# Causal attention with a soft mixture of experts: one transpose of the maxima for a pair of heads, and a rearranged opening

## Chip, cores and metric

The kernel runs on one core of one Trainium2 chip. The metric is the device time of one execution in microseconds (us). Before the change it is 418.62 us, the median of three runs (418.21 to 418.80).

## What is computed

The inputs q, k and v have 8 batches of 12 heads, 448 positions and 64 channels, in float32. A causal attention comes first; its result, with the heads side by side, is x of 3584 rows by 768. A soft mixture of 8 experts with 4 slots each follows.

```python
scores = scale * np.matmul(q, k.transpose(0, 1, 3, 2))
scores = np.where(mask, -1000000000.0, scores)      # mask: above the diagonal
scores = scores - np.max(scores, axis=-1, keepdims=True)
attn = np.exp(scores)
attn = attn / (np.sum(attn, axis=-1, keepdims=True) + 1e-09)
x = np.matmul(attn, v)
...
logits = x @ phi
d = softmax of logits over the rows; slot_input = d.T @ x
slot_out[e] = np.maximum(slot_input[e] @ w1[e], 0.0) @ w2[e]
c = softmax of logits over the slots; out = c @ slot_out
```

## The kernel before

The 96 heads are taken as 48 pairs. `block(p)` (from line 507) is the work around pair p: the last step of the scores of its heads a = 2p and a + 1, the first steps of the scores of the next pair's heads a + 2 and a + 3, and the attention's product with v for pair p. Every instruction is kept in the order in which the program is written, on its own engine (`_InOrder`, line 55), so the order of the calls in `block` is the order in each engine's queue. All instructions therefore carry line 65 in the profile; the tile names tell them apart.

The scores stand transposed in PSUM, keys on the partitions, one 1024-column tile `s` per head, three of them in turn. A head's way through the engines, by the names of functions and tiles:

- `cast_q`, `cast_k` (ScalarE) round q and k to the matmul's type into `qd` and `ks`; `sub_q`, `sub_k` (GpSimd, a few at the start on VectorE) put the rounding's remainder into the upper partitions of `r2` and `ks`; `copy_k2` (ScalarE) copies the rounded keys into `k2`. Remainder and rounded part together make the product exact enough.
- `scores1` (line 249, TensorE): six matmuls. The parts "c03" and "c12" add the causal mask with a bf16 identity (`s<-tri,identb`, 192 and 256 columns), the parts "k3" to "k0" are the product of 64, 192, 320 and 448 columns (`s<-qd,ks`). `scores1_all` fixes their order.
- `max_keys` (line 279, VectorE): k = 0 is the large transposing maximum of the 1024 columns of `s` (`TRANSPOSE_TENSOR_REDUCE r<-s`), k = 1 and 2 are two small maxima over blocks of keys (`TENSOR_REDUCE r<-r`).
- `max_row` (line 300): k = 0 transposes the tile `r` on TensorE (`rt<-ident,r`), k = 1 takes the last maximum of four groups, negated, on VectorE (`mr<-rt`). `rt` and the transposed x (`xm`) share one PSUM bank.
- `max_spread` (line 311, GpSimd): spreads `mr` by a select onto 14 rows of `r2` (`r<-mr` in the profile).
- `scores2` (line 322, TensorE): four matmuls (`s<-r,k`) that subtract the maximum and add the remainders; then `exps` (ScalarE, `pt<-s`).
- `attv` and `attv3` (TensorE, `po<-va,pt`): the product with v. `attv` is called once per head for the first three blocks of queries, `attv3` does the last block for both heads. `norm` (VectorE) divides by the sum into `x`.

In a steady block TensorE's queue is: scores2 of a, scores1 of a + 2, scores2 of a + 1, scores1 of a + 3, attv of a, rt of a + 2, attv of a + 1, attv3, rt of a + 3, then pieces of the mixture (its logits, or the products for the slots, another kind in each of six consecutive blocks), then the four transposes `xm` of the pair before. VectorE's is: the last of `norm` for the pair before, the three `max_keys` of a + 2, the large one of a + 3, mr of a + 2, the small two of a + 3, mr of a + 3, the first steps of `norm`, the mixture's sums. GpSimd's is: sub_q, sub_k, the two spreads.

Behind the last block the expert weights that did not fit beside the attention are loaded, and the experts and the combination run (from line 699). Lines 173 to 181 and 474 to 505 are the opening: the first loads, the first heads' work, and matmuls without use (`warm`, line 213) in the waits.

Of the kernel before, what the change touches and what calls it, by code (L numbers as in the profile page):

```python
# [9 lines left out]
F32 = mybir.dt.float32  # L10
# [16 lines left out]
NQB = S // 32  # L27
# [4 lines left out]
NHD = 2 * NPAIR  # L32
NR, XB, XT = 2, 3, 2
# [2 lines left out]
HT = 2  # L36
WN, PAD = 1536, 168
WARM = (2, 5, 2, 3, 3)
START = (8, 4)


FILL = 9
# [3 lines left out]


SC0, SC1, SC2, SC3 = 576, 0, 320, 512
RW, RC, RF = 96, 4, 20
NQ = 2 * NCH - 1  # L50
CQ0 = (0, 128, 256, 384)
SCOL = (SC0, SC1, SC2, SC3)
# [28 lines left out]
def attention_soft_moe(ctx: ExitStack, tc: tile.TileContext, qk, va, phi, w1, w2, out):  # L81
    nc = _Core(tc)
# [18 lines left out]
    r2_ = [fix.tile([P, 2, S], F32R, name="r20")]  # L101
# [4 lines left out]
    r_ = [fix.tile([P, RW], F32, name=f"r{i}") for i in range(2)]  # L106
# [11 lines left out]

    st = {}

    def load_qk(p, a, hs=slice(0, 2)):
        if p < NPAIR:
            if hs.start == 0:

                st["raw", a, p] = (wres.tile([P, 2 * WN], F32, tag="w", name=f"qk{a}_{p}")[:, 0:2 * S]
                                   .rearrange("p (h s) -> p h s", h=2)
                                   if (p, a) in ((1, 0), (2, 1)) else
                                   raw.tile([P, 2, S], F32, tag="qk", name=f"qk{a}_{p}"))
            nc.sync.dma_start(out=st["raw", a, p][:, hs], in_=qk[p, :, a, hs])

    def loads_v(p, eng=nc.sync):
        if p < NPAIR:
# [39 lines left out]

    for hs in (slice(0, 1), slice(1, 2)):
        load_qk(0, 1, hs)
        load_qk(0, 0, hs)
    load_qk(1, 1)
    load_qk(1, 0)
    loads_v(0)
    load_qk(2, 1)
    load_qk(2, 0)  # L180
# [22 lines left out]
    for i in range(NR):  # L203
        nc.gpsimd.memset(r2_[i][0:64, :, :].bitcast(F32), 0.0)
        nc.vector.memset(ks_[i][:, 2 * S:2 * S + KP].bitcast(F32), 0.0)
        nc.vector.memset(r_[i], -3.0e38)
# [36 lines left out]
    def sub_q(p, hs=slice(0, 2), eng=None):  # L243
        if p < NPAIR:
            (eng or nc.gpsimd).tensor_tensor(out=r2_[p % NR][64:P, hs], in0=st["raw", 0, p][64:P, hs],
                                             in1=qd_[p % NR][64:P, hs], op=ALU.subtract)


    def scores1(i, part):
        if i >= NHD:  # L250
            return
        p, h = divmod(i, 2)
        ks, qd = ks_[p % NR], qd_[p % NR]
        if ("s", i) not in st:
            st["s", i] = s_[i % 3]
            st["open"] = set()
        s = st["s", i]

        bank = part in ("c12", "k1", "k2")
        start = bank not in st["open"]  # L260
        st["open"].add(bank)
        if part[0] == "k":
            c = int(part[1])
            o, w, m = S * h + P * c, S - CQ0[c], min(P, S - P * c + (KP if i else 0))
            nc.tensor.matmul(s[0:m, SCOL[c]:SCOL[c] + w], ks[:, o:o + m],
                             qd[:, h, CQ0[c]:S], start=start, stop=False, skip_group_check=True)
            return
        if part == "c12":
            o = s[:, SC1:SC1 + 2 * SC2].rearrange("p (a n) -> p a n", n=SC2)[:, :, 0:P]
            mask = tri.unsqueeze(1).to_broadcast([P, 2, P])  # L270
        else:
            o, mask = s[:, SC3:SC3 + AW + P], tri2
        nc.tensor.matmul(o, identb, mask, start=start, stop=False, skip_group_check=True)

    def scores1_all(i):
        for part in ("c03", "c12", "k3", "k2", "k1", "k0"):
            scores1(i, part)

    def max_keys(i, k):

        if i >= NHD:
            return
        r = r_[i % 2]
        if k == 0:
            nc.vector.tensor_reduce(out=r[:, RC:RC + 72].rearrange("p (a b)->p a b", b=36)[:, :, 0:16],
                                    in_=st["s", i].rearrange("p (a b k)->p a b k", a=2, k=32),
                                    axis=AX.X, op=ALU.max, apply_transpose=True)  # L290
        elif k == 1:
            w = r[:, 0:84].rearrange("p (j q)->p q j", j=2)[:, 0:16]
            nc.vector.tensor_reduce(out=r[:, RF:RF + 76].rearrange("p (a q)->p a q", a=2)[:, :, 0:8],
                                    in_=w.rearrange("p (a q) j->p a q j", a=2), axis=AX.X, op=ALU.max)
        else:
            nc.vector.tensor_reduce(out=r[:, RF + 8:RF + NQB],
                                    in_=r[:, 14:80].rearrange("p (j q)->p q j", j=3)[:, 0:6],
                                    axis=AX.X, op=ALU.max)

    def max_row(i, k, w=RW - RF, to=None):  # L300
        if i >= NHD:
            return
        if k == 0:
            st["rt", i] = misc(f"rt{i}") if to is None else to
            nc.tensor.transpose(out=st["rt", i][0:w, 0:P], in_=r_[i % 2][:, RF:RF + w], identity=ident)
        else:
            mr = st["mr", i] = wk.tile([NQB, 32], F32, tag="mr", name=f"mr{i}", bufs=2)
            nc.vector.tensor_reduce(out=mr, in_=st.pop(("rt", i))[0:NQB, 0:P].rearrange("p (g t)->p t g", g=4),
                                    axis=AX.X, op=ALU.max, negate=True)

    def max_spread(i):
        if i >= NHD:
            return
        p, h = divmod(i, 2)
        mr = st.pop(("mr", i))

        nc.gpsimd.affine_select(out=r2_[p % NR][0:NQB, h].rearrange("p (b t)->p b t", t=32),
                                in_=mr.unsqueeze(1).to_broadcast([NQB, NQB, 32]),
                                compare_op=ALU.is_equal, fill=0.0, base=0,
                                pattern=[[-1, NQB], [0, 32]], channel_multiplier=1)  # L320

    def scores2(i, cs):
        if i >= NHD:
            return
        p, h = divmod(i, 2)
        s = st["s", i]
        k2, r2 = k2_, r2_[p % NR]
        for c in cs:
            o, w, m = S * h + P * c, S - CQ0[c], min(P, S - P * c + (KP if i else 0))
# [152 lines left out]
        nc.vector.memset(t, v)  # L482
    sub_q(0, h0)
    scores1_all(0)
    warm(START[1])
    for k in range(3):
        max_keys(0, k)
    cast_k(0, h1)
    cast_q(0, h1)
    sub_k(0, h1)  # L490
    nc.gpsimd.memset(si, 0.0)
    max_row(0, 0)
    max_row(0, 1)
    max_spread(0)
    scores1_all(1)
    cast_k(1, h0)
    cast_k(1, h1)
    cast_q(1, h0)
    sub_k(1, h0)
    sub_k(1, h1)  # L500
    for k in range(3):
        max_keys(1, k)
    sub_q(0, h1, nc.vector)
    for hf in range(2):
        nc.sync.dma_start(out=phis[hf], in_=phi[:, 3 * hf:3 * hf + 3])

    def block(p):
# [18 lines left out]
            xcopy(p - 2)  # L526
        scores1_all(a + 2)
        if p == 0:
            max_row(1, 0)
            max_row(1, 1)  # L530
            max_spread(1)
        for k in range(3):
            max_keys(a + 2, k)
        if p == 0:
# [3 lines left out]
        if p == 0:  # L538
            cast_k(2, h1)
        scores1_all(a + 3)  # L540
        max_keys(a + 3, 0)
        sub_q(p + 1)
        load_qk(p + 3, 0)
        if p:
            sub_k(p + 2)
            load_qk(p + 4, 1)
        if m6 == 2 and p > 6:
            logits_d(b, lt)
        copy_k2(p + 1)
# [16 lines left out]
            return  # L566
        for h in range(2):
            attv(a + h, [(qc, 3 * h + qc, FULL) for qc in range(3)], po2, begun)
            if h == 0:
                max_row(a + 2, 0, AW)  # L570
        max_row(a + 2, 1)
        max_spread(a + 2)
        for k in (1, 2):
            max_keys(a + 3, k)
        if p == 0:
            sub_k(2, eng=nc.vector)
            load_qk(4, 1)
# [351 lines left out]
```

## Time and profile before

| | before |
|---|---|
| median of three runs | 418.62 us |
| the profiled execution: time, span | 418.81 us, 417.1 us |
| mean granted TensorE clock | 0.974 |
| busy: TensorE, its weight load | 383.6 us (92%), 300.0 us (72%) |
| busy: VectorE, ScalarE, GpSimd | 295.2, 283.0, 263.3 us (71, 68, 63%) |
| opening: first scores2 of pair 0, of pair 1 | 9.66 us, 20.57 us |
| six consecutive steady blocks (107.57 to 145.81 us) | 38.24 us |
| from 318 us to the end (417 us) | DMA share about 1, 399 to 416 GB/s |

The span is the time from the first to the last instruction on the core; the execution's own time is 1.7 us longer. Busy shares are means over stages with different limits, so the stages are read apart. In rows of the timeline the first two numbers are start and length in us; a bracket at the end has the idle time of that engine just before, and what ended it. Rows with several instructions show the first one's shape. A matmul's end is modelled, so the starts are what counts on TensorE.

### The profile page before, as it was taken

The numbers are of one execution on the slowest core, as the hardware profiler recorded it, in microseconds if no ns is written. First come the engines' busy times: TensorE is split into PE (matmuls) and PEld (weight loads), VectorE is DVE, ScalarE is ACT, GpSimd is POOL, SyncE is SP. The second block draws the span as 40 slices with busy tenths as digits, with TensorE's granted clock in tenths as the row PEclk, the third lists the DMA queues.
The fourth block names the chain that finished last, engine by engine and source line by source line (L and its number), as shares of the span: only waits on it lengthen the run. The fifth ranks groups of instructions, "written<-read, shape, count | busy, mean of one in ns | idle before, by whom it ended". The sixth has DMA issues, their size and how long they took to land.

```text
span 417.1 us, 14076 instructions
## 1 busy us (share of the span) xinstructions
PE 383.6 (92%) x5710; PEld 300.0 (72%) x5710; DVE 295.2 (71%) x827; ACT 283.0 (68%) x402; POOL 263.3 (63%) x212
## 2 busy tenths in 40 slices
PE   7799999999999999999999999999998998997840
PEld 3678888888887888888888878888886644633420
DVE  6687777878877878888788778788884576433540
ACT  5677878877978888788779788887863111432430
POOL 6498898888888888988888888889862000000000
PEclk9699999999999999999999999999999999999975
DMA  7578787788777787677887777877849999999997
GB/s 275 183 228 263 251 261 224 256 260 270 236 232 243 254 283 242 224 257 247 261 270 238 230 242 255 291 236 245 278 156 415 405 426 427 421 417 415 397 394 319
DMA packets 34479, 119.16 MB, mean 286 GB/s; under 512 B 3824, under 2 KB 8944, under 8 KB 32880
## 3 DMA queue, kind: packets, MB, share of 16 engines
q1 hardware_dynamic: 34272, 118.01, 80.3%
q8 instruction: 45, 0.74, 0.7%
q10 hardware_dynamic: 144, 0.27, 0.2%
q14 instruction: 18, 0.15, 0.1%
HBM read 107.25 MB, written 11.01 MB: 284 GB/s over the span
## 4 chain that ended last, share of the span: by engine, by line
PE 78%; DVE 7%; DMA 5%; issue 3%; ACT 2%; POOL 1%; SPq 0%; DVEq 0%; POOLq 0%
PE s L65 34%; PE po L65 25%; PE xm L65 7%; PE rt L65 5%; DMA w<-in_w_dram 4%; PE so L65 2%; PE hp L65 2%; PE pp L65 2%; DVE lm L65 2%; DMA qk<-in_qk_dram 2%; DVE lg L65 1%; PE cp L65 1%; DVE r L65 1%; PE e L65 1%; DVE mr L65 1%
## 5 line engine op out<-in xcount | busy, mean ns | idle before, releaser
L65 ACT ACTIVATE pt<-s 128x1024 f32<-128x1024 f32 x96 | 98.8, 1030 | 53.5 <-PE s L65 49.9
L65 DVE TRANSPOSE_TENSOR_REDUCE r<-s 128x32 f32<-128x1024 f32 x96 | 119.5, 1245 | 20.9 <-PE s L65 18.4
L65 PE MATMUL po<-va,pt 128*64 128x65 f32 x3040 | 111.1, 226 | 0.0
L65 PEld LDWEIGHTS po<-va,pt 128*64 128x64 f32 x3040 | 97.8, 139 | 17.9 <-issue 11.9
L65 POOL TENSOR_TENSOR r<-qk,qd 64x896 fp32r<-64x896 f32 (+1 forms) x48 | 100.4, 2092 | 4.7 <-ACT qd L65 0.9
L65 POOL TENSOR_TENSOR ks<-qk,ks 64x896 fp32r<-64x896 f32 (+1 forms) x48 | 97.9, 2041 | 0.8 <-ACT ks L65 0.8
L65 POOL TENSOR_SCALAR_AFFINE_SELECT r<-mr 14x448 fp32r<-14x448 f32 x96 | 61.6, 642 | 46.2 <-DVE sm L65 26.6
L65 PE MATMUL s<-qd,ks 128*128 128x448 f32 (+4 forms) x384 | 79.8, 331 | 1.5 <-POOL ks L65 1.5
L65 PE MATMUL s<-r,k 128*128 128x448 f32 (+3 forms) x384 | 65.0, 292 | 1.4 <-POOL r L65 1.4
L65 PEld LDWEIGHTS s<-r,k 128*128 128x128 f32 (+1 forms) x384 | 59.6, 177 | 4.5 <-POOL r L65 2.3
L65 PEld LDWEIGHTS s<-qd,ks 128*128 128x128 f32 (+2 forms) x384 | 51.0, 180 | 1.7 <-POOL ks L65 1.7
L65 ACT ACTIVATE ks<-qk 128x896 fp32r<-128x896 f32 (+1 forms) x51 | 45.4, 892 | 3.7 <-DMA qk<-in_qk_dram 3.7
L65 ACT ACTIVATE qd<-qk 128x896 fp32r<-128x896 f32 (+1 forms) x50 | 46.1, 922 | 1.3
L65 ACT ACTIVATE k<-ks 64x896 fp32r<-64x896 f32 (+1 forms) x49 | 45.7, 934 | 1.1
L65 DVE TENSOR_REDUCE mr<-rt 14x32 f32<-14x128 f32 x96 | 24.8, 258 | 30.3 <-PE rt L65 30.3
L65 DVE TENSOR_REDUCE r<-r 128x16 f32<-128x32 f32 x192 | 33.7, 175 | 5.0
L65 PE MATMUL s<-tri,identb 128*128 128x192 bf16 x192 | 35.0, 264 | 0.0
L65 PE MATMUL xm<-ident,x 128*128 128x128 f32 x188 | 30.8, 286 | 3.4 <-DVE mr L65 3.4
L65 PEld LDWEIGHTS xm<-ident,x 128*128 128x128 f32 x188 | 19.7, 140 | 17.2 <-DVE sm L65 11.2
L65 PE MATMUL rt<-ident,r 128*64 128x128 f32 (+1 forms) x96 | 28.6, 298 | 1.7 <-DVE r L65 1.5
L65 ACT ACTIVATE xts<-xm 128x512 f32<-128x512 f32 x47 | 27.8, 592 | 0.2 <-PE xm L65 0.2
L65 DVE TENSOR_TENSOR x<-po,sm 128x384 f32<-128x384 f32 (+2 forms) x49 | 26.4, 540 | 0.4
(138 smaller groups left out, 355.8 us busy)
## 6 DMA issues: line engine op xcount, KB each, us to landing
qk<-in_qk_dram SPq DMA_DIRECT2D x94, 448.0 KB, 4.2
w<-in_w_dram SPq DMA_DIRECT2D x43, 768.0 KB, 7.2
w<-in_w_dram SPq DMA_DIRECT2D x10, 1536.0 KB, 20.1
va<-in_va_dram SPq DMA_DIRECT2D x47, 260.0 KB, 4.5
out_dram<-ot SPq DMA_DIRECT2D x16, 384.0 KB, 6.7
out_dram<-ot SPq DMA_DIRECT2D x2, 1536.0 KB, 9.2
qk<-in_qk_dram SPq DMA_DIRECT2D x4, 224.0 KB, 3.3
hw<-in_w_dram SPq DMA_DIRECT2D x1, 768.0 KB, 7.5
```

The source lines that it names most:

```text
L65: return self._tc.keep_in_program_order(op(*args, **kwargs))
```

## The change

The maxima of both heads of a pair go into one tile `r`, first head's 14 columns at 0, second head's at 32. One transpose and one small maximum `mr` serve the pair, on 46 partitions; `max_spread` is called for each head. The one `max_row` stands behind both calls of `attv` and ahead of `attv3`, and all three `max_keys` of the second head come ahead of it. On TensorE, the piece of a steady block from the product with v to the next block, before (pt_99 and pt_101 are the two heads' exponentials):

```order
L65 MATMUL po<-va_100,pt_99 64x65 x12
L65 MATMUL rt_364<-ident,r_95 64x128
L65 MATMUL po<-va_100,pt_101 64x65 x12
L65 MATMUL po<-va_100,pt_99 64x65
...
L65 MATMUL rt_391<-ident,r_96 64x128
L65 MATMUL xm_399<-ident,x_104 128x128 x4
L65 MATMUL s_86<-r_90,k_97 128x448
```

And now (the heads' exponentials are pt_98 and pt_100):

```order
L65 MATMUL po<-va_99,pt_98 64x65 x12
L65 MATMUL po<-va_99,pt_100 64x65 x12
L65 MATMUL rt_375<-ident,r 64x128
L65 MATMUL po<-va_99,pt_98 64x65
...
L65 MATMUL xm_392<-ident,x_103 128x128 x4
L65 MATMUL s_86<-r_90,k_96 128x448
```

The rows left out are the other seven of `attv3`. One rt is gone, and the other stands between `attv` of the second head and `attv3`. On VectorE, in the same block, before:

```order
L65 TENSOR_REDUCE r_95<-s_86 128x2x16
L65 TENSOR_REDUCE r_95<-r_95 128x2x8
L65 TENSOR_REDUCE r_95<-r_95 128x6
L65 TENSOR_REDUCE r_96<-s_87 128x2x16
L65 TENSOR_REDUCE mr_378<-rt_364 14x32
L65 TENSOR_REDUCE r_96<-r_96 128x2x8
L65 TENSOR_REDUCE r_96<-r_96 128x6
L65 TENSOR_REDUCE mr_393<-rt_391 14x32
L65 TENSOR_SCALAR sm_396<-po 128x7
```

And now:

```order
L65 TENSOR_REDUCE r<-s_86 128x2x16
L65 TENSOR_REDUCE r<-r 128x2x8
L65 TENSOR_REDUCE r<-r 128x6
L65 TENSOR_REDUCE r<-s_87 128x2x16
L65 TENSOR_REDUCE r<-r 128x2x8
L65 TENSOR_REDUCE r<-r 128x6
L65 TENSOR_REDUCE mr_377<-rt_375 46x32
L65 TENSOR_SCALAR sm_389<-po 128x7
```

The first `mr` is gone, and the remaining one comes after both heads' maxima. The masks of `scores1_all` change their order on TensorE; before:

```order
L65 LDWEIGHTS identb
L65 MATMUL s_85<-tri_129,identb 128x192
L65 LDWEIGHTS identb
L65 MATMUL s_85<-tri_129,identb 128x2x128
L65 MATMUL s_85<-qd_91,ks_92 66x64
L65 MATMUL s_85<-qd_91,ks_92 128x192
```

And now:

```order
L65 LDWEIGHTS identb
L65 MATMUL s_85<-tri_128,identb 128x192
L65 MATMUL s_85<-qd_91,ks_92 66x64
L65 LDWEIGHTS identb
L65 MATMUL s_85<-tri_128,identb 128x2x128
L65 MATMUL s_85<-qd_91,ks_92 128x192
```

The product of 64 columns moved between the two masks. In the opening, the first loads of q go through ScalarE's queue, those of k stay on SyncE's; the first heads take 64 rows instead of 66 for that small product, so that they need only their own half of `ks`; sub_q and sub_k of pairs 1 and 2 are done by halves; the pair's transpose is done twice for pair 0, once for each head; and filler matmuls go into the bank `po`. The clearing of `si` on GpSimd moves from the opening to block 4. The diff, cut to its core:

```diff
-START = (8, 4)
+START = (8, 2, 2, 3)
-RW, RC, RF = 96, 4, 20
+RW, RC, RH = 244, 68, 52
...
     for hs in (slice(0, 1), slice(1, 2)):
         load_qk(0, 1, hs)
-        load_qk(0, 0, hs)
+        load_qk(0, 0, hs, nc.scalar)
     load_qk(1, 1)
-    load_qk(1, 0)
+    load_qk(1, 0, eng=nc.scalar)
...
-            o, w, m = S * h + P * c, S - CQ0[c], min(P, S - P * c + (KP if i else 0))
+            o, w, m = S * h + P * c, S - CQ0[c], min(P, S - P * c + (KP if i > 4 or i % 2 else 0))
...
-        for part in ("c03", "c12", "k3", "k2", "k1", "k0"):
+        for part in ("c03", "k3", "c12", "k2", "k1", "k0"):
...
-            nc.tensor.transpose(out=st["rt", i][0:w, 0:P], in_=r_[i % 2][:, RF:RF + w], identity=ident)
+            nc.tensor.transpose(out=st["rt", p][0:AW, 0:P], in_=r_[:, 0:AW], identity=ident)
...
+            mr = st["mr", p] = wk.tile([AW, 32], F32, tag="mr", name=f"mr{p}", bufs=2)
+            nc.vector.tensor_reduce(out=mr[0:32 + NQB], axis=AX.X, op=ALU.max, negate=True,
+                                    in_=st.pop(("rt", p))[0:32 + NQB, 0:P].rearrange("p (g t)->p t g", g=4))
...
     scores1_all(0)
-    warm(START[1])
+    warm(START[1], pob)
...
-    nc.gpsimd.memset(si, 0.0)
+    sub_q(0, h1, nc.vector)
+    scores1_all(1)
     max_row(0, 0)
     max_row(0, 1)
-    max_spread(0)
-    scores1_all(1)
...
     sub_k(1, h0)
+    max_spread(0, 0)
+    warm(START[2], pob)
     sub_k(1, h1)
     for k in range(3):
         max_keys(1, k)
-    sub_q(0, h1, nc.vector)
...
         if p == 0:
-            max_row(1, 0)
-            max_row(1, 1)
-            max_spread(1)
+            max_row(0, 0)
+            max_row(0, 1)
+            max_spread(0, 1)
+            warm(START[3], pob)
+        elif p == 4:
+            nc.gpsimd.memset(si, 0.0)
...
-        max_keys(a + 3, 0)
+        for k in range(3):
+            max_keys(a + 3, k)
...
         for h in range(2):
             attv(a + h, [(qc, 3 * h + qc, FULL) for qc in range(3)], po2, begun)
-            if h == 0:
-                max_row(a + 2, 0, AW)
-        max_row(a + 2, 1)
-        max_spread(a + 2)
-        for k in (1, 2):
-            max_keys(a + 3, k)
+        max_row(p + 1, 0)
+        max_row(p + 1, 1)
+        for h in range(2):
+            max_spread(p + 1, h)
         if p == 0:
-            sub_k(2, eng=nc.vector)
-            load_qk(4, 1)
+            sub_k(2, h1)
         attv3(p)
-        max_row(a + 3, 0, AW)
-        max_row(a + 3, 1)
-        max_spread(a + 3)
```

More of the change, by code (lines that the diff above doesn't have):

```diff
@@ L105, in attention_soft_moe @@
     x_[1] = fix.tile([P, NCH, 3 * P], F32, name="x1")
-    r_ = [fix.tile([P, RW], F32, name=f"r{i}") for i in range(2)]
+    r_ = fix.tile([P, RW], F32, name="r")
     k2_ = fix.tile([P, 2 * S + KP], F32R, name="k2")
@@ L119, in attention_soft_moe, with load_qk @@
     st = {}
-    def load_qk(p, a, hs=slice(0, 2)):
+    def load_qk(p, a, hs=slice(0, 2), eng=nc.sync):
         if p < NPAIR:
@@ L128, in load_qk @@
                                    raw.tile([P, 2, S], F32, tag="qk", name=f"qk{a}_{p}"))
-            nc.sync.dma_start(out=st["raw", a, p][:, hs], in_=qk[p, :, a, hs])
+            eng.dma_start(out=st["raw", a, p][:, hs], in_=qk[p, :, a, hs])
     def loads_v(p, eng=nc.sync):
@@ L205, in attention_soft_moe @@
         nc.vector.memset(ks_[i][:, 2 * S:2 * S + KP].bitcast(F32), 0.0)
-        nc.vector.memset(r_[i], -3.0e38)
+    nc.vector.memset(r_, -3.0e38)
     nc.vector.memset(k2_[0:64, 0:2 * S].bitcast(F32), 1.0)
@@ L285, in max_keys @@
             return
-        r = r_[i % 2]
+        r, f = r_[:, RC + RH * (i % 2) - 4:], r_[:, 32 * (i % 2):]
         if k == 0:
-            nc.vector.tensor_reduce(out=r[:, RC:RC + 72].rearrange("p (a b)->p a b", b=36)[:, :, 0:16],
+            nc.vector.tensor_reduce(out=r[:, 4:64].rearrange("p (a b)->p a b", a=2)[:, :, 0:16],
                                     in_=st["s", i].rearrange("p (a b k)->p a b k", a=2, k=32),
@@ L291, in max_keys @@
         elif k == 1:
-            w = r[:, 0:84].rearrange("p (j q)->p q j", j=2)[:, 0:16]
-            nc.vector.tensor_reduce(out=r[:, RF:RF + 76].rearrange("p (a q)->p a q", a=2)[:, :, 0:8],
+            n = RC + 18 + (RH - 32) * (i % 2)
+            w = r[:, 0:72].rearrange("p (j q)->p q j", j=2)[:, 0:16]
+            nc.vector.tensor_reduce(out=f[:, 0:2 * n].rearrange("p (a q)->p a q", a=2)[:, :, 0:8],
                                     in_=w.rearrange("p (a q) j->p a q j", a=2), axis=AX.X, op=ALU.max)
@@ L295, in max_keys, with max_row @@
         else:
-            nc.vector.tensor_reduce(out=r[:, RF + 8:RF + NQB],
-                                    in_=r[:, 14:80].rearrange("p (j q)->p q j", j=3)[:, 0:6],
+            nc.vector.tensor_reduce(out=f[:, 8:NQB], in_=r[:, 14:38].rearrange("p (j q)->p q j", j=3)[:, 0:6],
                                     axis=AX.X, op=ALU.max)
-    def max_row(i, k, w=RW - RF, to=None):
-        if i >= NHD:
+    def max_row(p, k):
+        if p >= NPAIR:
             return
         if k == 0:
-            st["rt", i] = misc(f"rt{i}") if to is None else to
-            nc.tensor.transpose(out=st["rt", i][0:w, 0:P], in_=r_[i % 2][:, RF:RF + w], identity=ident)
-        else:
-            mr = st["mr", i] = wk.tile([NQB, 32], F32, tag="mr", name=f"mr{i}", bufs=2)
-            nc.vector.tensor_reduce(out=mr, in_=st.pop(("rt", i))[0:NQB, 0:P].rearrange("p (g t)->p t g", g=4),
-                                    axis=AX.X, op=ALU.max, negate=True)
@@ L311, in max_spread @@
-    def max_spread(i):
-        if i >= NHD:
+            st["rt", p] = misc(f"rt{p}")
+            nc.tensor.transpose(out=st["rt", p][0:AW, 0:P], in_=r_[:, 0:AW], identity=ident)
+        else:
+            mr = st["mr", p] = wk.tile([AW, 32], F32, tag="mr", name=f"mr{p}", bufs=2)
+            nc.vector.tensor_reduce(out=mr[0:32 + NQB], axis=AX.X, op=ALU.max, negate=True,
+                                    in_=st.pop(("rt", p))[0:32 + NQB, 0:P].rearrange("p (g t)->p t g", g=4))
+    def max_spread(p, h):
+        if p >= NPAIR:
@@ L313, in max_spread @@
             return
[L314 to L318, printed above, removed]
+        mr, r = st["mr", p], slice(32 * h, 32 * h + NQB)
+        nc.gpsimd.affine_select(out=r2_[p % NR][r, h].rearrange("p (b t)->p b t", t=32),
+                                in_=mr[r].unsqueeze(1).to_broadcast([NQB, NQB, 32]),
                                 compare_op=ALU.is_equal, fill=0.0, base=0,
@@ L328, in scores2 @@
         for c in cs:
-            o, w, m = S * h + P * c, S - CQ0[c], min(P, S - P * c + (KP if i else 0))
+            o, w, m = S * h + P * c, S - CQ0[c], min(P, S - P * c + (KP if i > 4 or i % 2 else 0))
             nc.tensor.matmul(s[0:m, SCOL[c]:SCOL[c] + w], k2[:, o:o + m],
@@ L540, in block @@
         scores1_all(a + 3)
-        max_keys(a + 3, 0)
-        sub_q(p + 1)
-        load_qk(p + 3, 0)
+        for k in range(3):
+            max_keys(a + 3, k)
         if p:
+            sub_q(p + 1)
+            load_qk(p + 3, 0)
             sub_k(p + 2)
-            load_qk(p + 4, 1)
+        else:
+            sub_q(1, h0)
+            sub_k(2, h0)
+            sub_q(1, h1)
+            load_qk(3, 0)
+        load_qk(p + 4, 1)
         if m6 == 2 and p > 6:
```

## Prediction

> **What bounds the kernel now.** I read the page first. Its parts 1 and 2 show TensorE busy in nine tenths of nearly every slice up to 300 us, and in part 4 the chain that ended last is TensorE for 78% of the span. Then I read a table by stage, cut at the first `s<-r,k` matmul of six consecutive blocks (pairs 17 to 22 of 48):
>
> ```profile
> 122.86:129.16 6.30, 6.30 (x110) 5.42 (x108) 5.18 (x16) 5.17 (x6) 5.46 (x5) 1.00 0.87 286
> 129.16:135.67 6.51, 6.51 (x101) 5.21 (x100) 4.97 (x15) 5.17 (x6) 5.64 (x5) 1.00 0.68 218
> 135.67:141.96 6.29, 6.29 (x109) 5.41 (x108) 5.30 (x15) 5.17 (x6) 5.28 (x4) 1.00 0.88 302
> 141.96:148.21 6.25, 6.02 (x95) 5.23 (x94) 5.40 (x17) 5.45 (x9) 5.40 (x5) 1.00 0.62 192
> 148.21:154.80 6.59, 6.59 (x117) 5.70 (x116) 4.86 (x14) 5.93 (x10) 5.69 (x5) 1.00 0.89 298
> 154.80:161.09 6.29, 6.29 (x101) 5.21 (x100) 5.24 (x16) 5.18 (x6) 5.27 (x4) 1.00 0.67 215
> ```
>
> The columns are length, busy time of TensorE, its weight load, VectorE, ScalarE and GpSimd, then clock, DMA share and GB/s. TensorE has no idle time in five of six blocks. But VectorE has 5 us of work in 6.3, and whether it has slack depends on where in the block its work must be finished. For that the timeline of the first of these blocks, TensorE first, then VectorE and GpSimd (start, length):
>
> ```profile
> 122.86 0.71 PE L65 MATMUL s<-r,k 128*128 128x448 f32 x4
> 123.42 0.36 PE L65 MATMUL s<-tri,identb 128*128 128x192 bf16 x2
> 124.19 0.63 PE L65 MATMUL s<-r,k 128*128 128x448 f32 x4
> 124.69 0.35 PE L65 MATMUL s<-tri,identb 128*128 128x192 bf16 x2
> 125.55 0.92 PE L65 MATMUL po<-va,pt 128*64 128x65 f32 x24
> 126.40 0.30 PE L65 MATMUL rt<-ident,r 128*64 128x128 f32 x1
> 126.62 1.39 PE L65 MATMUL po<-va,pt 128*64 128x65 f32 x40
> 127.94 0.30 PE L65 MATMUL rt<-ident,r 128*64 128x128 f32 x1
> 128.17 0.65 PE L65 MATMUL s<-xts,phi 128*32 128x128 f32 x16
> 128.75 0.66 PE L65 MATMUL xm<-ident,x 128*128 128x128 f32 x4
> ...
> 124.39 1.25 DVE L65 TRANSPOSE_TENSOR_REDUCE r<-s 128x32 f32<-128x1024 f32 x1 [0.30 <-PE s L65]
> 125.99 1.24 DVE L65 TRANSPOSE_TENSOR_REDUCE r<-s 128x32 f32<-128x1024 f32 x1
> 127.15 0.24 DVE L65 TENSOR_REDUCE mr<-rt 14x32 f32<-14x128 f32 x1
> 127.32 0.38 DVE L65 TENSOR_REDUCE r<-r 128x16 f32<-128x32 f32 x2
> 128.35 0.28 DVE L65 TENSOR_REDUCE mr<-rt 14x32 f32<-14x128 f32 x1 [0.66 <-PE rt L65]
> ...
> 128.70 0.64 POOL L65 TENSOR_SCALAR_AFFINE_SELECT r<-mr 14x448 fp32r<-14x448 f32 x1 [0.59 <-DVE sm L65]
> ```
>
> There is a ring through two engines. The block's first scores2 (122.86) is followed by scores1 of the next pair's first head; its large maximum starts 1.53 later (124.39). From there VectorE works without a gap on both heads' maxima until 127.32 + 0.38 = 127.70, which is 3.31 later. The second head's rt transpose comes at 127.94, and 1.22 after it the next block begins (129.16). How long rt needs after the last small maximum is seen in the opening, where TensorE waits for it:
>
> ```profile
> 7.75 0.39 DVE L65 TENSOR_REDUCE r<-r 128x16 f32<-128x32 f32 x2
> 8.29 0.28 PE L65 MATMUL rt<-ident,r 128*76 128x128 f32 x1 [0.96 <-DVE r L65]
> ```
>
> 8.29 - (7.75 + 0.39) = 0.15. So the ring needs 1.53 + 3.31 + 0.15 + 1.22 = 6.21 us, and TensorE's own work 6.30. VectorE is 0.09 us away from being the bound. The change must be judged by this ring, not by TensorE's busy time alone.
>
> **The change part by part.** *One transpose for a pair.* TensorE loses one rt: 126.40 to 126.62, 0.22 us a block. VectorE loses one mr, but that one lay where the first small maximum waited for the large one anyway: a large maximum to its first small one takes 125.99 to 127.32, 1.33 us, with mr between, and 1.31 without:
>
> ```profile
> 13.22 1.23 DVE L65 TRANSPOSE_TENSOR_REDUCE r<-s 128x32 f32<-128x1024 f32 x1
> 14.48 0.40 DVE L65 TENSOR_REDUCE r<-r 128x16 f32<-128x32 f32 x2
> ```
>
> This start has 1.26, so I take a gain of 0.02, with 0.07 as the other end. What matters is the new place. The one rt needs both heads' maxima and stands ahead of attv3, which stood ahead of the late rt before. TensorE takes its matmuls in order, so attv3, the logits, xm and the next block are queued behind it, and all engines wait for that block. attv3 thus moves into the ring. It is 16 of the 40 `po` records: (127.94 - 126.62) - (126.40 - 125.55) = 1.32 - 0.85 = 0.47 us.
>
> *Masks in another order.* After the first mask now comes the 64-column product, then the second mask, so the 192-column product's weights load under a 256-column mask, not under 64 columns. A load of such weights and of a mask's:
>
> ```profile
> L65 PEld LDWEIGHTS s<-qd,ks 128*128 128x128 f32 x288 | 40.4, 194 | 0.0
> L65 PEld LDWEIGHTS <-identb 128*128 128x128 bf16 x211 | 14.1, 100 | 2.3 <-issue 1.7
> ```
>
> At best one load of 0.19 us disappears; at worst the extra change between types costs a mask load, 0.10. I take a gain of 0.08, as only part of the 0.19 can be exposed: scores1 takes 0.77 (123.42 to 124.19) for 1472 columns, scores2 0.56 for 1024, so there is little idle time in it to remove. In the ring it counts once a block, since the second scores1 lies beside VectorE's first head.
>
> *The ring after.* 1.53 - 0.08 = 1.45; 3.31 - 0.02 = 3.29; 0.15; and from rt to the next block 0.22 + 0.47 + logits 0.58 (128.17 to 128.75) + xm 0.41 (128.75 to 129.16) = 1.68. Sum 6.57, 0.27 more than now. TensorE's own work would be 6.30 - 0.22 - 0.16 = 5.92, so it should stand idle for about 0.65 us before each rt.
>
> The six kinds of block differ in what stands for "logits". Three (6.30, 6.51 and 6.29 in the first, second and sixth row) take +0.27. In the third (6.29) the logits' maximum and its update sit on VectorE ahead of x; with attv3 earlier than the logits they end after scores1: +0.07 more, 0.34. In the fourth (6.25) there are only two transposes, half of xm's 0.41; there GpSimd's spread for the first head is last: 128.35 - 127.94 = 0.41, mr 0.28, 0.07 to the spread, 0.64, and about 0.05 to TensorE, in all 1.45, against 0.22 + 0.47 + 0.20 + 0.41 = 1.30. Its ring is 1.45 + 3.29 + 0.15 + 1.45 = 6.34, +0.10 rounded. The fifth (6.59) waits for VectorE already now, since its late rt comes 5.16 after its start where the first block's came 5.08 after: +0.19.
>
> ```profile
> 153.37 0.30 PE L65 MATMUL rt<-ident,r 128*64 128x128 f32 x1
> ```
>
> Together 3 x 0.27 + 0.34 + 0.10 + 0.19 = 1.44 per six blocks. Blocks 7 to 46 are 6.67 such sixes: +9.6. Blocks 3 to 6 have less between rt and xm: 2 x 0.10 + 2 x 0.27 = +0.7. Blocks 1 and 2 took 6.6 each in the opening's wake and take some 6.35: -0.5. In sum +9.8 us.
>
> Two spreads in a row on GpSimd cost nothing: 2 x 0.64 and two subtractions of 2.1 fit into 6.5 (5.3 to 5.7 busy in the table), and the second head's product comes over 1 us after the first's.
>
> *The opening.* Here the changed code should gain. The rows of now:
>
> ```profile
> 0.80 1.28 ACT L65 ACT_TABLE_LOAD   x1 [0.80 <-PEq L917]
> 0.81 2.76 SPq L65 DMA_DIRECT2D qk<-in_qk_dram  x6
> 9.09 1.05 ACT L65 ACTIVATE ks<-qk 128x448 fp32r<-128x448 f32 x2 [2.16 <-DMA qk<-in_qk_dram]
> 9.80 2.23 POOL L65 TENSOR_TENSOR ks<-qk,ks 64x448 fp32r<-64x448 f32 x2 [0.19 <-ACT ks L65]
> 12.08 0.79 PE L65 MATMUL s<-qd,ks 128*66 128x64 f32 x4 [1.48 <-POOL ks L65]
> 14.06 1.22 PE L65 MATMUL s<-r,k 128*128 128x448 f32 x4 [1.08 <-POOL r L65]
> 20.57 0.59 PE L65 MATMUL s<-r,k 128*128 128x448 f32 x2
> ```
>
> Six loads on SyncE take 2.76, 0.46 each; the keys of pair 1 go from fifth to third on their queue, 0.95 earlier. They are what ScalarE waits for at 9.09. Since scores1 of head 2 now needs only the first half of the subtraction (two columns fewer), it saves a further 1.1 (half of 2.23) of the 12.08. Against that, the first spread waits behind that half, ScalarE starts its table 1.3 later behind its own three loads, and block 1's first maximum has to wait for the second head's. Following the queues in order, with the durations above: the keys land at 8.0, cast 8.6, first half subtracted 9.7, first spread 10.4, the first scores2 at 10.5 (now 9.66) and scores1 of head 2 behind it at 11.1 (now 12.08); head 1's maxima are done at 11.2, its rt 11.8, spread 12.5 to 13.15, its scores2 at 13.2 (now 14.06); scores1 of head 3 ends at 14.4, its maxima 1.95 later, rt 16.5, mr, spread, and block 1 starts at 17.95 where it stood at 20.57: -2.6 us. The ends: -3.6, if the waits for data fall away too, and -0.5, if the clock behaves as now:
>
> ```profile
> 6.37:9.78 3.41, 2.12 (x13) 1.09 (x13) 2.31 (x5) 1.25 (x3) 2.52 (x3) 1.00 1.01 391
> 9.78:13.19 3.41, 1.72 (x11) 1.10 (x11) 2.81 (x5) 3.31 (x6) 2.23 (x2) 1.00 0.98 363
> 13.19:16.60 3.41, 2.54 (x10) 2.13 (x10) 1.62 (x4) 1.43 (x3) 2.73 (x2) 0.50 0.75 269
> ```
>
> After a stretch with TensorE busy for 2.12 of 3.41 us the clock stayed full; after one with 1.72 it was half, for 6.8 us. With the fillers I count about 2.2 in that stretch, nearer to the first, so I take the full clock. The Trainium skill's page "TensorE: Matmul & The Clock Gate" (Part 1, the HAM clock gate) has the clock fall only after a whole idle window of about 3.4 us; no wait of 3.4 us is in that stretch, so the trace disagrees. By that rule the fillers could do nothing, and the opening would gain the lesser end. For the two queues the skill's first page, "Trainium Kernel Development and Optimization" (Key Constraints), says that queues of several engines share the same DMA engines and save only issue time; that is the 0.95 taken here, and more would need bandwidth that the 0.98 to 1.01 DMA share of these rows doesn't leave.
>
> *The end.* Nothing is changed behind the last pair:
>
> ```profile
> 318.00:344.00 26.00, 24.80 (x411) 15.30 (x414) 15.72 (x64) 4.25 (x14) 0.00 (x0) 1.00 1.02 416
> ```
>
> There the weights' loads fill the DMA (share 1.02) and begin when the attention's buffers come free, so a shift of the attention is a shift of the whole.
>
> Sum: +9.8 - 2.6 = +7.2. The profiled execution took 418.81 with a span of 417.1, so 424.3 and 426.0; the median of the runs, 418.62, is 0.2 less: 425.8 us.
>
> **The rivals.** *TensorE stays the bound* and the ring is hidden. Each block is then 0.38 shorter (0.22 + 0.16), 46 times 17.5, with the opening 20 us: about 398.5. For it speaks the busy table; against it that VectorE's last maximum ends 4.74 after the block's start (4.84 less 0.10) and lets rt go at 4.89, while TensorE reaches it at 126.40 + 0.85 - 0.16 - 122.86 = 4.23. It decides if that chain is 0.66 us shorter than traced, or if it waits less for a part I put in series: 7%. *The ring is longer, but cheaply:* with masks at 0.19 and the opening at 3.6 the sum is 418.6 + 9.8 - 5.1 - 3.6 = 419.7, near no change; only both extremes do that: 3%. *The fillers don't do what they say,* and the clock halves again: 427.9, in my range, and part of the forecast's 88%. *Short idles bring the clock down in every block:* 0.65 us of idle time per 6.57 leaves TensorE 90% busy, well over the 62% at which the rows kept it; if it fell in a tenth of the 46 blocks, at some 3 us a time, that is +14, 440: 2%. The Trainium skill's page on TensorE (A second HAM failure mode) has such oscillation from frequent short idles; no row here shows it above 62%.
>
> **How the numbers follow.** The forecast has 88%. Low end: opening -3.6 and masks 0.15 (46 x 0.07 = 3.2), 425.8 - 1.0 - 3.2 = 421.6. High end: opening -0.5 and a mask gain of 0.03 (2.3), 425.8 + 2.1 + 2.3 = 430.2. The two faster cases and the slow clock lie outside, with some tails. A measurement of this kernel tells 0.2% (0.8 us) from no change. Faster 8%, same 3%, slower 89%.
>
> **What would show it.** Right: blocks of about 6.55 us, an idle time of some 0.6 us before rt, released by VectorE's small maximum, block 1 at about 18 us with a full clock, and the tail as long as before. Wrong: if rt follows `po` without a wait, the ring is hidden and blocks take 5.9; if scores1 takes 0.8 or more, the masks cost instead of gaining; if block 1 starts after 20 us, the opening gave nothing.

## The result, and the profile after

| | before | after |
|---|---|---|
| median of the runs beside each other (us) | 418.71 (418.21 to 418.86, 4 runs) | 431.81 (431.42 to 432.46, 4 runs) |
| span of the profiled execution (us) | 417.1 | 429.9 |
| first scores2 of pair 0, pair 1, pair 47 (us) | 9.66, 20.57, 314.73 | 11.44, 18.97, 328.51 |
| mean granted TensorE clock | 0.974 | 0.984 |

The changed kernel takes 1.0317 of the time before, 95% interval 1.0299 to 1.0334. The forecast was 425.8 us with a range up to 430.2: the direction is right, and the size lies outside the range. The page of after:

```profile
span 429.9 us, 13850 instructions
...
PE 370.3 (86%) x5666; PEld 290.2 (68%) x5666; DVE 295.1 (69%) x778; ACT 283.6 (66%) x402; POOL 265.5 (62%) x215
...
PE 37%; DVE 34%; DMA 14%; issue 6%; ACT 3%; POOL 1%; DVEq 0%; POOLq 0%; SPq 0%
...
L65 PE MATMUL rt<-ident,r 128*64 128x128 f32 x49 | 13.4, 274 | 31.9 <-DVE r L65 31.9
```

TensorE works 13.3 us less than before (383.6) in a span 12.8 us longer. The chain that ended last was TensorE for 78%, and is now shared by TensorE (37%) and VectorE (34%). The last row is where they meet: TensorE stands idle for 31.9 us ahead of `rt`, and the maxima `r` on VectorE end that wait. The same six consecutive blocks as in the prediction's table (pairs 17 to 22), with the same columns:

```profile
125.69:132.39 6.70, 6.06 (x109) 5.26 (x107) 5.21 (x15) 5.17 (x6) 5.46 (x5) 1.00 0.87 278
132.39:139.28 6.89, 6.25 (x100) 5.03 (x99) 5.00 (x14) 5.17 (x6) 5.66 (x5) 1.00 0.61 190
139.28:145.96 6.68, 6.04 (x108) 5.25 (x107) 5.33 (x14) 5.17 (x6) 5.24 (x5) 1.00 0.90 291
145.96:152.47 6.51, 5.69 (x95) 5.10 (x93) 5.39 (x16) 5.72 (x10) 5.11 (x5) 1.00 0.54 171
152.47:159.44 6.97, 6.26 (x116) 5.47 (x115) 4.93 (x13) 5.78 (x10) 6.01 (x5) 1.00 0.83 275
159.44:166.13 6.69, 6.04 (x101) 5.04 (x99) 5.28 (x15) 5.17 (x6) 5.24 (x5) 1.00 0.65 214
```

The sum is 40.44, where it was 38.23 and the forecast 38.23 + 1.44 = 39.67. TensorE was busy through five of six blocks; now it lacks 0.64 to 0.71 us in five and 0.82 in the fourth. The first of these blocks, TensorE first, then VectorE:

```profile
125.69 0.71 PE L65 MATMUL s<-r,k 128*128 128x448 f32 x4
...
126.97 0.63 PE L65 MATMUL s<-r,k 128*128 128x448 f32 x4
...
128.32 1.62 PE L65 MATMUL po<-va,pt 128*64 128x65 f32 x48
130.58 0.27 PE L65 MATMUL rt<-ident,r 128*64 128x128 f32 x1 [0.64 <-DVE r L65]
130.78 0.69 PE L65 MATMUL po<-va,pt 128*64 128x65 f32 x16
131.40 0.65 PE L65 MATMUL s<-xts,phi 128*32 128x128 f32 x16
131.97 0.66 PE L65 MATMUL xm<-ident,x 128*128 128x128 f32 x4
132.39 0.71 PE L65 MATMUL s<-r,k 128*128 128x448 f32 x4
...
127.17 1.25 DVE L65 TRANSPOSE_TENSOR_REDUCE r<-s 128x32 f32<-128x1024 f32 x1 [0.24 <-PE s L65]
128.45 0.40 DVE L65 TENSOR_REDUCE r<-r 128x16 f32<-128x32 f32 x2
128.76 1.24 DVE L65 TRANSPOSE_TENSOR_REDUCE r<-s 128x32 f32<-128x1024 f32 x1
130.04 0.40 DVE L65 TENSOR_REDUCE r<-r 128x16 f32<-128x32 f32 x2
130.96 0.28 DVE L65 TENSOR_REDUCE mr<-rt 46x32 f32<-46x128 f32 x1 [0.53 <-PE rt L65]
131.52 0.17 DVE L65 TENSOR_SCALAR sm<-po 128x7 f32<-128x7 f32 x1 [0.27 <-PE po L65]
```

Read as the ring: 1.48 to the first large maximum, 3.27 for both heads' maxima (127.17 to 130.44), 0.14 to `rt`, in all 4.89. From `rt` to the next block it is 0.20 + 0.62 + 0.57 + 0.42 = 1.81. The first part is what the prediction had; in the second, attv3 (the `po` with 16 records at 130.78) takes 0.62 to the start of the next group, where the prediction had 0.47.

### The profile page after: what moved, and what is told of

Same layout as the page of the kernel before. It is cut to its first block, busy times and chain, and to the rows that moved or that the text cites. A ratio compares the mean times of both kernels' runs of the same rounds, so it can differ in the third digit from the quotient of the medians.

```text
span 429.9 us, 13850 instructions
## 1 busy us (share of the span) xinstructions
PE 370.3 (86%) x5666; PEld 290.2 (68%) x5666; DVE 295.1 (69%) x778; ACT 283.6 (66%) x402; POOL 265.5 (62%) x215
## 4 chain that ended last, share of the span: by engine, by line
PE 37%; DVE 34%; DMA 14%; issue 6%; ACT 3%; POOL 1%; DVEq 0%; POOLq 0%; SPq 0%
DVE r L65 32%; PE s L65 18%; DMA w<-in_w_dram 13%; PE po L65 7%; PE xm L65 5%; PE rt L65 3%; ACT pt L65 2%; PE pp L65 1%; DVE x L65 1%; POOL r L65 1%; PE hp L65 1%; DMA qk<-in_qk_dram 1%; PE e L65 1%; ACT xts L65 1%; ACT ot L65 0%
## 5 line engine op out<-in xcount | busy, mean ns | idle before, releaser
L65 PE MATMUL po<-va,pt 128*64 128x65 f32 x3040 | 109.7, 225 | 0.0
L65 PEld LDWEIGHTS po<-va,pt 128*64 128x64 f32 x3040 | 96.5, 137 | 17.5 <-issue 11.6
L65 POOL TENSOR_TENSOR ks<-qk,ks 64x896 fp32r<-64x896 f32 (+1 forms) x50 | 100.3, 2006 | 0.9 <-ACT ks L65 0.7
L65 PE MATMUL s<-qd,ks 128*128 128x448 f32 (+4 forms) x384 | 81.3, 323 | 0.7 <-DVE ks L65 0.7
L65 PEld LDWEIGHTS s<-qd,ks 128*128 128x128 f32 (+2 forms) x384 | 53.2, 185 | 1.9 <-ACT qd L65 1.3
L65 PE MATMUL rt<-ident,r 128*64 128x128 f32 x49 | 13.4, 274 | 31.9 <-DVE r L65 31.9
L65 PE MATMUL s<-tri,identb 128*128 128x192 bf16 x192 | 39.6, 271 | 0.0
L65 DVE TENSOR_REDUCE r<-r 128x16 f32<-128x32 f32 x192 | 34.9, 182 | 6.6
L65 DVE TENSOR_REDUCE mr<-rt 46x32 f32<-46x128 f32 x49 | 13.8, 282 | 25.6 <-PE rt L65 25.6
L65 PEld LDWEIGHTS rt<-ident,r 128*64 128x64 f32 x49 | 5.3, 109 | 37.2 <-PE po L65 37.1
```

Of the source, the lines that this page charges most:

```text
L65: return self._tc.keep_in_program_order(op(*args, **kwargs))
```

## The experiments

Two theories stood against each other for the 6 us beyond the forecast. *The ring:* what stands on TensorE behind the one `rt` counts in full, attv3 above all. *Other costs:* the new order of the masks, the two queues or the fillers lose time. All ratios are to runs of the kernel before on the same chip.

**attv3 ahead of the transpose.** In the changed kernel:

```
         for h in range(2):
             attv(a + h, ...)
+        attv3(p)
         max_row(p + 1, 0)
         max_row(p + 1, 1)
...
-        attv3(p)
```

> The changed kernel with attv3 moved ahead of the pair's rt transpose; all else as changed. Theory (ring): a block lasts as long as the way from its first scores2 over both heads' maxima to rt (4.89 us) and from rt to the next block. With attv3 out of the second part, that part is no longer 1.80 but the larger of 1.22 to 1.42 (rt, logits, xm) and 1.45 (maximum, spread on GpSimd), so 1.45: blocks of 6.34 instead of 6.69 on average, some 16 us less, about 415 to 417 us. Rival (the pair's late maxima alone cost it, wherever attv3 stands): the wait ahead of rt just gets shorter by what attv3 fills, the blocks stay at 6.6 to 6.7, 429 to 432 us.

Measured 416.88 us (416.24 to 417.65), 0.9961 of before (0.9947 to 0.9975): one moved call takes away all of the 13 us and more. A block of it, TensorE, then GpSimd:

```profile
123.83 2.09 PE L65 MATMUL po<-va,pt 128*64 128x65 f32 x64
126.09 0.27 PE L65 MATMUL rt<-ident,r 128*64 128x128 f32 x1 [0.18 <-DVE r L65]
126.29 0.64 PE L65 MATMUL s<-xts,phi 128*32 128x128 f32 x16
126.87 0.66 PE L65 MATMUL xm<-ident,x 128*128 128x128 f32 x4
127.52 0.74 PE L65 MATMUL s<-r,k 128*128 128x448 f32 x4
...
126.83 1.35 POOL L65 TENSOR_SCALAR_AFFINE_SELECT r<-mr 14x448 fp32r<-14x448 f32 x2 [0.74 <-DVE sm L65]
```

`rt` starts 4.90 after its block's start (121.19), as in the changed kernel. But the next block now comes 1.43 later, since only the spread of the first head is last: 126.83 and half of 1.35 is 127.51. From 121.19 to 159.28 six blocks take 38.09, five of them 6.33 to 6.35 and one 6.41; before the change the six took 38.23. And here is why the prediction's price was too low: 64 records of `po` in one run take 2.09, 48 take 1.62 (block above), so 16 more in a run cost 0.47. By themselves between other matmuls the same 16 took 0.62.

**A matmul without use, on either side of the wait.** One bf16 matmul of 512 columns a block, into a tile's part that nothing reads then:

```
+        warm(1, s_[(a + 1) % 3][:, 512:1024])     # e6: here
         max_row(p + 1, 0)
...
         attv3(p)
+        warm(1, s_[(a + 1) % 3][:, 512:1024])     # e7: here instead
```

> The changed kernel with one matmul of 512 columns in bf16 more in every block (it writes a bank that is overwritten later; the result does not use it), just ahead of the pair's rt. In the opening such a matmul takes 0.22 us at full clock, here perhaps 0.3 with its weights. Theory (ring): it lies in the wait ahead of rt (0.64 us) and costs nothing: 431.3 to 432.5. Rival (TensorE's own work still counts): 46 times 0.22 to 0.3, 442 to 446.

> The same matmul, behind attv3 instead. Theory (ring): it lies between rt and the next block and counts in full in the blocks that do not wait for the spread: 46 times 0.22 to 0.3, 440 to 446. Rival (GpSimd's spread, 1.45 us behind rt, sets the next block in most blocks): at most a third of that, 431.5 to 435.

Ahead of `rt`, 431.62 us (431.42 to 433.24), 1.0327 (1.0302 to 1.0352): free. Behind attv3, 443.66 us (443.2 to 445.2), 1.061 (1.0588 to 1.0632): 11.9 us more than the changed kernel. First the kernel with it ahead, then with it behind:

```profile
128.28 1.62 PE L65 MATMUL po<-va,pt 128*64 128x65 f32 x48
129.83 0.39 PE L65 MATMUL s<-tri,identb 128*128 128x512 bf16 x1
130.54 0.27 PE L65 MATMUL rt<-ident,r 128*64 128x128 f32 x1 [0.32 <-DVE r L65]
```

```profile
134.97 0.27 PE L65 MATMUL rt<-ident,r 128*64 128x128 f32 x1 [0.63 <-DVE r L65]
135.17 0.69 PE L65 MATMUL po<-va,pt 128*64 128x65 f32 x16
135.79 0.39 PE L65 MATMUL s<-tri,identb 128*128 128x512 bf16 x1
136.11 0.64 PE L65 MATMUL s<-xts,phi 128*32 128x128 f32 x16
```

Ahead, the wait shrinks from 0.64 to 0.32 and the blocks stay at 6.69. Behind, the wait stays at 0.63 and the blocks take 7.01, longer by 136.11 - 135.79 = 0.32. (Only the fourth row's kind grows by less, 6.68 for 6.50, since TensorE was not last there. From block 1 to block 47 this profile has 341.87 - 19.76 = 322.1 us for 309.5, the 12.6 that 46/6 x (5 x 0.32 + 0.18) = 13.6 lets expect within 1 us.) It is the same instruction; its place relative to the wait decides. attv3 still takes 0.62 (135.17 to 135.79), with a bf16 matmul behind it.

**The masks.** Once alone on the kernel before, once taken back in the changed kernel:

```
-        for part in ("c03", "c12", "k3", "k2", "k1", "k0"):     # e2: - to +
+        for part in ("c03", "k3", "c12", "k2", "k1", "k0"):     # e5: + to -
```

> The kernel before with nothing changed but the order of the masks. In the changed kernel's trace a scores1 is about 0.06 shorter. Theory: before, TensorE is the bound, but its second scores1 already waits for the exponentials of the first head, so only the second one's gain is kept: 0.06 to 0.07 in each of 46 blocks, some 3 us less, 415.5 us (414.5 to 416.5). Rival 1: both count, 0.13 a block, 412.7. Rival 2: the gain is lost to the next wait of VectorE, 418 to 419.

> The changed kernel with the masks in the old order. Theory (ring): the first scores1 of a block lies in the ring, and its 0.06 is lost in each of 46 blocks: 2.9 us more, 434 to 435.5. Rival (TensorE is idle ahead of rt anyway, so its own work does not count): 431.5 to 432.5.

Alone, 415.81 us (415.23 to 416.39), 0.994 (0.9921 to 0.9958): 2.8 us less than the 418.62 of the runs of before beside it, and blocks of 6.23 for 6.29. Taken back, 435.29 us (434.36 to 437.25), 1.041 (1.0381 to 1.0439), and blocks of 6.76 for 6.69. So the order of the masks is a gain, about 0.06 a block in both, and not the cause.

**The opening's parts.** No fillers, and all first loads on SyncE's queue:

```
-START = (8, 2, 2, 3)
+START = (8, 0, 0, 0)                       # e4
...
-        load_qk(0, 0, hs, nc.scalar)
+        load_qk(0, 0, hs)                  # e3, and load_qk(1, 0) likewise
```

> The changed kernel without its seven filler matmuls behind the first scores; the eight at the very start stay. Theory (the fillers keep the clock): the clock is half for 6.8 us once more in the opening, and the time is 1 to 3 us longer, 433 to 435. Rival (the waits there are too short to matter, or VectorE bounds that stretch): clock full as in the changed kernel or halved without effect, 431.5 to 432.

> The changed kernel with all first loads on the SyncE queue again. Theory (two queues delay what is needed first): with two queues the first half of k lands 1.1 us later than before, since it shares the DMA engines with q from the start, and ScalarE's table load comes 1.4 later; with one queue the first scores2 comes up to 1 us earlier, 430.8 to 431.5. Rival (the earlier keys of pair 1 are worth more): those come 0.95 later again and the first spread waits behind them, 432 to 433.

Without fillers 434.15 us (433.91 to 435.61), 1.0381 (1.0359 to 1.0402), 2.3 more than with them. On one queue 431.97 us (430.87 to 433.05), 1.0321 (1.0295 to 1.0348): no difference can be seen. The table by stage of the kernel without fillers, then of the changed one:

```profile
5.40:8.81 3.41, 1.71 (x12) 1.23 (x12) 3.03 (x10) 2.62 (x6) 2.47 (x3) 1.00 1.04 417
8.81:12.22 3.41, 1.49 (x10) 1.31 (x8) 2.09 (x5) 0.75 (x3) 3.07 (x3) 0.50 1.02 368
...
15.63:19.04 3.41, 3.41 (x41) 2.97 (x42) 1.53 (x3) 2.95 (x4) 2.53 (x3) 0.50 0.00 0
19.04:22.45 3.41, 2.87 (x50) 2.50 (x47) 1.77 (x7) 1.87 (x3) 1.92 (x3) 1.00 0.25 68
```

```profile
10.34:13.75 3.41, 2.35 (x15) 1.48 (x14) 2.50 (x6) 1.51 (x2) 2.09 (x3) 1.00 0.97 337
```

Without fillers the clock halves at 8.81, after 3.41 us with TensorE busy for 1.71 (before: after 1.72), and stays half for 10.2 us. In the changed kernel's trace the busy time is 2.35 and the clock stays full. But the fillers do not rule the fall out: of nine profiled executions with them, three have the half clock in the opening all the same, for 6.8 us (the old masks above), 3.4 us (the matmul behind attv3) and 3.4 us (the first kernel of the next experiment), after 3.41 us with 1.29, 1.60 and 0.80 us of work. The mean clocks of the single executions fit: 0.970 to 0.972 in the four without fillers, 0.977 to 0.984 in the four of the changed kernel.

**The opening without the new transpose.** The kernel before, with the new masks, START of the changed kernel and the order of its opening (edits of `scores1`, `scores2`, lines 474 to 505 and `block(0)`), but a transpose for each head in the old places: once on one queue, and, since the changed kernel's trace on one queue (block 1 at 18.09, and at 18.97 on two) suggested a loss by the two, then side by side on two and on one.

```
-        load_qk(0, 0, hs)                  # e8 and e10: one queue
+        load_qk(0, 0, hs, nc.scalar)       # e9: two queues, load_qk(1, 0) likewise
```

> The kernel before with the new order of masks and with the changed opening (halves, fillers, the smaller product, the clearing moved), but one queue for the first loads, and in the steady blocks a transpose for each head as before. Theory: blocks as with the masks alone (415.8 us), and the opening earlier by what the changed kernel with one queue shows, block 1 at 18.1 instead of 19.9: 414.0 (413.3 to 414.8). Rival (what the opening gains is lost in blocks 1 and 2, where the queues catch up): 415.5 to 416.5.

> The best version so far (the kernel before with new masks and the changed opening) with the first loads on two queues as in the change. Theory (two queues delay the first half of k by sharing the DMA engines with q): block 1 starts 0.9 us later than with one queue, as the traces of the changed kernel with two queues and with one show (18.97 against 18.10): 415.5 us against 414.6. Rival (the difference between those traces was chance): the same as with one queue within 0.3 us.

> The same with one queue, once more beside it on the same chip: 414.3 to 414.9 us; the theory puts it 0.9 below the run with two queues, the rival at the same time.

On one queue 414.61 us (414.48 to 414.66), 0.9909 (0.9894 to 0.9923). Then two queues 413.56 us (412.87 to 413.99), 0.9881 (0.9861 to 0.9901), and one again 414.50 us (413.36 to 415.87), 0.9911 (0.989 to 0.9932). That two queues lose time has fallen; whether they gain up to 1 us stays unclear, as the intervals overlap. What is clear is that the changed opening and the masks beat the kernel before, by 0.9 to 1.2%, and that the pair's transpose in its new place costs about 431.81 - 413.56 = 18 us against that. Even with attv3 moved ahead of it (416.88, 0.9947 to 0.9975 of before), the pair's one transpose stays behind the two transposes of this kernel on the same two queues (0.9861 to 0.9901).

## Why the prediction was wrong in size

Its sum against the two traces, by starts of blocks:

| stretch | forecast | measured |
|---|---|---|
| start to block 1 | -2.6 | 18.97 - 20.57 = -1.6 |
| block 1 to block 47 | +9.8 | 309.54 - 294.16 = +15.4 |
| block 47 to the end | 0 | 101.4 - 102.4 = -1.0 |
| sum | +7.2 | +12.8 |

**The blocks: the failed step.** "attv3 thus moves into the ring. It is 16 of the 40 `po` records: (127.94 - 126.62) - (126.40 - 125.55) = 1.32 - 0.85 = 0.47 us." The mechanism is right, the size is not: that difference is what 16 records add to a longer run of the same shape, and behind the `rt` they stand alone. There they take 0.62, so `rt` to the next block is longer by 0.59 and not by 0.46: in the block above 1.81 and not 1.68. Five of six kinds of block have it; by their lengths it is 5 x 0.12 = 0.60 per six blocks. The prediction's own two rows held the missing piece: 24 records took 0.85, but at 0.47 for 16 they would take 0.71, so each group has 0.14 us of its own, and 0.47 + 0.14 = 0.61 is what stood there after the change. What this beginning of a group consists of, no run here shows.

The other part is VectorE's own queue, which the prediction followed for the third row only. For the fourth it took the first block's 1.45 from the block's start to the large maximum. But in that kind of block VectorE comes to the maximum late, and did so before the change: the update of the logits' maximum (`run_m`, at 142.41 before and 146.41 now) and the end of `norm` (`x`) stand ahead of it. Before, then now:

```profile
143.00 0.57 DVE L65 TENSOR_SCALAR x<-po,sm 64x64 f32<-64x64 f32 x2
143.60 1.25 DVE L65 TRANSPOSE_TENSOR_REDUCE r<-s 128x32 f32<-128x1024 f32 x1
```

```profile
147.00 0.57 DVE L65 TENSOR_SCALAR x<-po,sm 64x64 f32<-64x64 f32 x2
147.60 1.25 DVE L65 TRANSPOSE_TENSOR_REDUCE r<-s 128x32 f32<-128x1024 f32 x1
```

Both times the large maximum starts when `x` is done, 1.64 after the block's start (141.96 and 145.96), where the first block's has 1.48 now. What the masks save on TensorE does not count there, and `rt` comes 0.17 late. That makes the fourth row +0.26 instead of +0.10; in the fifth `rt` is 0.07 late, and in the third the 0.07 that the prediction added did not come. In sum 0.60 + 0.16 + 0.07 - 0.07 = 0.76, and 40.44 - 39.67 is 0.77. Over blocks 7 to 46 the miss is (328.51 - 58.33) - (314.73 - 58.88) - 9.6 = 4.7 us. The other 0.8 or so lies in blocks 1 to 6: blocks 1 and 2 took 32.13 - 18.97 = 13.16 for 33.80 - 20.57 = 13.23, where 0.5 less was forecast, and blocks 3 to 6 came out 1.1 longer instead of 0.7.

Why the range did not hold it: its high end moved the opening and the masks to their bounds, but this term had none, being taken for a row of the trace. A second row for it, or the idea that a group has a beginning, would have given 46 x 0.15 = 7 us more at the high end.

**What held.** From block start to `rt` 4.89 forecast and 4.89 measured, of which both heads' maxima are 3.27 for 3.29 (the prediction's "1.31 without" is not what the rows beside it give, 14.48 - 13.22 = 1.26; now a large maximum to its first small one takes 130.04 - 128.76 = 1.28); an idle time of 0.6 us before `rt`, released by VectorE's small maximum (0.64); the spread's 1.45 from `rt` to the next block where TensorE is not last (1.43 with attv3 moved, and 151.02 to 152.47 in the fourth row's block). The masks gained 0.06 to 0.07 for 0.08. They count once a block in the ring, as said, and in the fourth row's kind not at all (6.50 to 6.51 with either order). The dummy matmul on either side of the wait shows the ring in both directions.

**The rivals.** *TensorE stays the bound* fell with the waits at `rt`, and *the ring is longer, but cheaply* with the masks' 0.06 and the opening's 1.6. *Short idles bring the clock down* did not come: the clock is 1.00 in all six rows, with TensorE busy for 0.87 to 0.91 of them; so the oscillation that the Trainium skill describes on its page "TensorE: Matmul & The Clock Gate" (A second HAM failure mode) is not to be seen at 0.64 us of idle time per block. *The fillers don't do what they say* fell for the changed kernel: taking them out costs 2.3 us. That they always keep the clock is not so, as told above. That page's rule (Part 1, the HAM clock gate), by which the clock falls after a whole idle window of about 3.4 us, does not fit these traces: it halved after stretches with 1.71 and 1.72 us of work in 3.41, the longest wait ahead of the fall being 1.22 in the kernel without fillers, and 2.61 in all six traces in which it fell in the opening.

**The opening** gained 1.6 instead of 2.6 in this trace, and the missing 1.0 is there at the first scores2 already (11.44 for 10.5). Its rows, all engines in order of time:

```profile
2.21 1.28 ACT L65 ACT_TABLE_LOAD   x1 [2.21 <-issue]
4.49 0.58 ACT L65 ACTIVATE ks<-qk 128x448 fp32r<-128x448 f32 x1 [0.67 <-DMA qk<-in_qk_dram]
8.01 1.04 ACT L65 ACTIVATE ks<-qk 128x448 fp32r<-128x448 f32 x2 [0.82 <-DMA qk<-in_qk_dram]
8.22 1.20 PE L65 MATMUL s<-qd,ks 128*128 128x192 f32 x3
8.67 1.14 POOL L65 TENSOR_TENSOR ks<-qk,ks 64x448 fp32r<-64x448 f32 x1 [0.73 <-ACT ks L65]
8.99 1.30 DVE L65 TENSOR_TENSOR r<-qk,qd 64x448 fp32r<-64x448 f32 x1
9.23 0.41 PE L65 MATMUL rt<-ident,r 128*64 128x128 f32 x1
10.32 0.28 DVE L65 TENSOR_REDUCE mr<-rt 46x32 f32<-46x128 f32 x1
10.74 0.65 POOL L65 TENSOR_SCALAR_AFFINE_SELECT r<-mr 14x448 fp32r<-14x448 f32 x1 [0.93 <-DVE mr L65]
11.44 0.73 PE L65 MATMUL s<-r,k 128*128 128x448 f32 x4 [0.96 <-POOL r L65]
12.19 0.70 PE L65 MATMUL s<-qd,ks 128*128 128x192 f32 x3
```

The keys of pair 1 are cast at 8.01, as forecast (8.0), and the half that GpSimd subtracts is done at 8.67 + 1.14 = 9.81 (forecast 9.7). But the spread behind it starts only at 10.74, because it waits for `mr`. VectorE does sub_q first (8.99, 1.30), as the new order has it, so `mr` starts 1.09 after `rt` (10.32 and 9.23), where before it started 0.32 after (8.61 and 8.29). The prediction followed GpSimd's queue there and not VectorE's.

`rt` itself is 0.94 later than before. The first cast begins 1.1 later than before (3.37) and waits for its load, not for the table. And TensorE still works at half speed: the three products at 8.22 take 1.20, the same three at 12.19 take 0.70, while before the change the first head's four products took 1.42 at 5.01 and the second's already 0.81 at 8.52. (The clock column of the stages reads 1.00 in this first stretch, and the mean of 0.984 leaves it out.) In the kernel without fillers, whose first cast is as late (4.50) but whose products run at full speed (0.71 for three of them at 5.97), the first head's large maximum begins at 6.77 instead of 7.28, and its `rt` stands at 8.67.

How much of this belongs to the queues is open. The changed kernel on one queue has the first cast at 3.42, the first scores2 at 10.55 and block 1 at 18.09, nearly as forecast (10.5 and 17.95), but its median is no shorter; and with this opening and the old transposes on one queue the first cast began at 3.55 (the last run above), and that kernel was no faster than the one on two. The page "Trainium Kernel Development and Optimization" of the Trainium skill (Key Constraints) allows several queues a saving of issue time only, and the runs agree in so far as no more than 1 us of it can be seen.

**The end** was 1.0 us shorter, with the same 399 matmuls in its first 26 us and the same busy time. In traces of kernels with the same code there it took 101.4 to 102.4 us, whatever the blocks did, so I take it for spread; what sets it was not tried.

## What to carry to other kernels

When an operation is merged or moved, write down the ring through the engines that wait for each other, and sort TensorE's instructions into those ahead of the wait (free, as far as the wait reaches) and those between it and the next block (paid in full): a dummy instruction on either side shows in two runs which is which. Price a moved group as it will stand, not as the difference between two runs of its kind. A busy share of 92% on one engine does not mean that its savings count: this change took 13 us of work from TensorE and made the kernel 13 us slower.

## What the runs showed that was not expected

- A short group of matmuls has a beginning: 16 records of `po` cost 0.47 us in a run of 64 and 0.62 between other matmuls, with an f32 or a bf16 group behind them.
- The clock falls with the amount of work in a stretch, and not for one long wait. In the six traces in which it fell in the opening, TensorE had worked for 0.80 to 1.72 of the 3.41 us ahead of the fall. In all other stretches of the opening at full clock (cut in steps of 3.41 us from the first change of the clock on) it worked for 1.89 us or more, and the clock held. The longest wait does not tell them apart: it was 1.22 us ahead of one fall, and up to 1.51 us where the clock held. The clock came back after 3.4, 6.8 or 10.2 us.
- The opening differs from trace to trace of the same code: on one queue, with the same loads in the same order, block 1 began at 19.00 in one profile and at 18.08 in the other, with medians of 414.61 and 414.50. In the first the clock was half from 12.17 to 15.58, in the second it stayed full. A single trace does not settle a microsecond there.
